# Tile-by-tile start, a 12-head last out-projection chunk and deadline-driven fillers in a one-core attention kernel

One core of one Trainium2 chip. The metric is the device time of one execution in microseconds. Profiles are of single executions; their spans run some 1.7 to 1.9 us under the times of the same executions.

## The reference

A LayerNorm without gain feeds two branches: attention of 32 heads over given key and value caches with an output projection, and an MLP with squared ReLU. Cut to what matters:

```python
# x: [2048, 512] bf16; k_cache, v_cache: [32, 2048, 128]; wq: [512, 4096]; wo: [4096, 512]
# w1: [512, 1792]; w2: [1792, 512]
xn = layernorm(x)
q = heads(xn @ wq)                                  # 32 heads of 128
p = softmax(q @ k_cache.T * 128 ** -0.5)
s = concat_heads(p @ v_cache) @ wo
g = silu(square(relu(xn @ w1 + b1)) @ w2 + b2)
out = x + s * g
```

## The kernel before

Queries are taken in four blocks of 512. A head of a block is eight *steps*; a step makes scores for two key tiles (2 matmuls of 512 columns), one exponential on ScalarE, and, two steps later, the product with V (8 matmuls of 129 columns, "PV"). Everything else of TensorE, called *fillers* here, is put between: projections of later heads (4 matmuls), MLP jobs (4 or 14), out-projection jobs over chunks of 8 heads. A credit counter spreads them. Cut, with `...` for what is left out:

```python
for i in range(TPB):                    # the four x tiles, all on SyncE
    ln_load(0, i)
fill_k(0)                               # a transposing DMA load, 512 KB
fill_wq(0, AC); fill_wq(1, AC); fill_v(0, AC); fill_wq(2, AC); fill_v(1, AC)    # ScalarE's queue
warm_up(10)
...                                     # norms on VectorE, transposes on TensorE
fill_k(1)
...                                     # w1 in four loads on SyncE, then b1 and b2 on GpSimd
for g in range(2):                      # heads 0 and 1 projected whole
    n, mm, evac = job_proj(g)
    for i in range(n):
        mm(i, g)
    t_bankF[g] = evac(g, 0)
t_b1 = E(DV, partial(_copy, out=b1f[:], in_=b1b[:]), deps=[tok_b1])
...
for pi in range(NPAIR):                 # 1024 steps
    gen_scores(pi)
    credit = min(credit + left[0] / (NPAIR - pi), 8.0)
    ...                                 # up to 2 or 3 fillers: fill_one(pi)
    if pi >= LAG:
        gen_pv(pi - LAG)
    ...
# last chunk of 8 heads: all heads but the last of every tile first, then the last heads
for i, (_, _, (n, mm, evac)) in enumerate(tail):
    for x in range(n - 1):
        mm(x, (places[i], waits[i]))
for i, (_, _, (n, mm, evac)) in enumerate(tail):
    mm(n - 1, (places[i], waits[i]))
    evac((places[i], waits[i]), step)
```

Names in the profiles: PE is TensorE (PEld its weight loads), DVE VectorE, ACT ScalarE, POOL GpSimd, SPq SyncE's queue of instructions. Tiles: `x_ln` x, `wq_sb` and `w_sb` weights (w1 and w2 are both `w_sb`), `kT` transposed keys, `v_sb` values, `qt_sb` projected queries, `oT` the transposed output of a head, which a transposing DMA makes. `psA`, `psF` and `psO`, in PSUM, are what the matmuls write: scores (2048 matmuls into `psA` in the page of the changed kernel), fillers (1460 into `psF`, the warm-up left out) and PV (8192 into `psO`). An *evacuation* is a copy out of PSUM. The *granted clock* is the share of TensorE's full speed that it was given. The *DMA share* adds up the packets' times over 16 DMA engines; it passes 1 (1.37 from 10 to 12 us in the kernel before).

The softmax here doesn't subtract the row's maximum and nothing guards it: scores larger than these inputs give would overflow.

Of the kernel before, what the change touches and what calls it, by code (L numbers as in the profile page):

```python
# [180 lines left out]

def _recip(e, out, in_):
    return e.reciprocal(out, in_)  # L183
# [36 lines left out]
def bass_recurrent_scan__mha_block_cached__dense_activation_squared_relu__prompt_kernel(  # L220
# [30 lines left out]
    NCH = H // HC  # L251
    LAG = 2
# [37 lines left out]
    mv_t = sb("mv_t", [P, TPB, 2], F32)  # L290
    ve_t = sb("ve_t", [P, TPB], F32)
# [31 lines left out]
    t_warm = E(GP, partial(_memset, out=warm[:], val=0.0))  # L323
# [15 lines left out]
    def ln_load(j, i):  # L339
        jt = j * TPB + i  # L340
        t_xl[jt] = S.emit_dma(
            SP, partial(_dma, out=x_ln[:, i, :], in_=A_x[0, jt * P:(jt + 1) * P, :]), sl_xl[i],
            deps=[t_xn.get(jt - TPB)])

    def ln_stats(j, i):
        jt = j * TPB + i
        prev = [t_xn.get(jt - TPB), t_xr.get(jt - TPB)]
        t = E(DV, partial(_bn_stats, out=st_t[:, i, :], in_=x_ln[:, i, :]),
              deps=[t_xl[jt]] + prev)
        t = E(DV, partial(_bn_aggr, out=mv_t[:, i, :], in_=st_t[:, i, :]), deps=[t])  # L350
        t = E(DV, partial(_ts, out=ve_t[:, i:i + 1], in0=mv_t[:, i, 1:2], scalar1=LN_EPS,
                          scalar2=None, op0=ALU.add), deps=[t])
        t_xr[jt] = E(GP, partial(_tt, out=rstd[:, i:i + 1], in0=ve_t[:, i:i + 1], in1=mhalf[:],
                                 op=ALU.pow), deps=[t, t_mhalf] + prev)

    def ln_scale(j, i):
        jt = j * TPB + i
        t_xn[jt] = E(DV, partial(_ts, out=xn_t[:, i, :], in0=x_ln[:, i, :],
                                 scalar1=mv_t[:, i, 0:1], scalar2=rstd[:, i:i + 1],
                                 op0=ALU.subtract, op1=ALU.mult),  # L360
                     deps=[t_xr[jt], t_xnr.get(jt - TPB)])
        if j > 0:
            t_xnr[jt] = tok_xT[j][i] = S.emit_dma(
                SP, partial(_dmaT, out=xnT[:, :, jt * P:(jt + 1) * P], in_=xn_t[:, i, :]),
                sl_xT[i], deps=[t_xn[jt]])
            return
        view = psA[:, i * 512:i * 512 + 256].bitcast(BF16)
        for c in range(NDC):
            t = E(PE, partial(_peT, out=view[:, c * P:(c + 1) * P],
                              in_=xn_t[:, i, c * P:(c + 1) * P], ident=ident[:]),  # L370
                  deps=[t_xn[jt], t_ident], inc=(c == NDC - 1))
        t_xnr[jt] = t
        tok_xT[0][i] = E(AC, partial(_act, out=xnT[:, :, i * P:(i + 1) * P],
                                     in_=view.rearrange("p (c q) -> p c q", q=P),
                                     func=ACT.Copy), deps=[t])

    def warm_up(n):
        for _ in range(n):
            E(PE, partial(_mm, out=bankF(1), lhsT=warm[:, 0:P], rhs=warm[:], start=True,
                          stop=True), deps=[t_warm], inc=False)  # L380
# [106 lines left out]
    def gen_oT(g):  # L487
        chunk = g // HC
        tok_oT[g] = S.emit_dma(
            SP, partial(_dmaT, out=oT[:, g % NOT, :].rearrange("p (t q) -> p t q", q=P),  # L490
                        in_=o_bf[:, g % 2, :, :].rearrange("p t d -> p (t d)")), sl_oT[g % 4],
            deps=[t_onorm[g], t_wodone.get(chunk - NOT // HC)])
# [47 lines left out]
    def job_h(j, c):  # L540
# [8 lines left out]
        def evac(bank, step):  # L549
            s = c % 2  # L550
            t1 = E(DV, partial(_ts, out=r_t[:, s, :], in0=bankF(bank), scalar1=b1f[:, c:c + 1],
                               scalar2=0.0, op0=ALU.add, op1=ALU.max),
                   deps=[box[0], t_b1, t_rt[s]])
            t_h2[j, c] = t_rt[s] = E(
                DV, partial(_tt, out=h2T[:, c, :], in0=r_t[:, s, :], in1=r_t[:, s, :],
                            op=ALU.mult),
                deps=[t1] + [t_o2.get((j - 1, qt)) for qt in range(TPB)])
            return t1
# [35 lines left out]
    def job_wo(j, m, qt):  # L594
        jt = j * TPB + qt
        g0 = j * H + m * HC
        box = [None]

        def mm(n, bank):
            g = g0 + n  # L600
            place, free = (bankF(bank), t_bankF[bank]) if isinstance(bank, int) else bank
            box[0] = E(PE, partial(_mm, out=place,
                                   lhsT=oT[:, g % NOT, qt * P:(qt + 1) * P],
                                   rhs=wo_all[:, m * HC + n, :], start=(n == 0),
                                   stop=(n == HC - 1)),
                       deps=[tok_wo[m], tok_oT[g], free], inc=(n == HC - 1))

        def evac(bank, step):
            if qt == TPB - 1:
                t_wodone[j * NCH + m] = box[0]  # L610
            if m == 0:
                t_acc[qt] = t = E(DV, partial(_copy, out=acc[:, qt, :], in_=bankF(bank)),
                                  deps=[box[0], t_fin.get(jt - TPB)])
            elif m < NCH - 1:
                t_acc[qt] = t = E(DV, partial(_tt, out=acc[:, qt, :], in0=bankF(bank),
                                              in1=acc[:, qt, :], op=ALU.add),
                                  deps=[box[0], t_acc[qt]])
                if m == NCH - 2:
                    at(step + 1, partial(pre_combine, j, qt))
            else:  # L620
                s = jt % 2
                place = bankF(bank) if isinstance(bank, int) else bank[0]
                t = E(DV, partial(_stt, out=tmp_t[:, s, :], in0=place, scalar=0.5,
                                  in1=g_all[:, jt % (2 * TPB), :], op0=ALU.mult, op1=ALU.mult),
                      deps=[box[0], t_g[jt], t_tmp[s]])
                t_fin[jt] = t_tmp[s] = E(
                    DV, partial(_tt, out=out_t[:, s, :], in0=tmp_t[:, s, :], in1=acc[:, qt, :],
                                op=ALU.add), deps=[t, t_u[jt], t_outdma[s]])
                eng, sl = (SP, sl_fin) if j == NQB - 1 else (GP, sl_out)
                t_outdma[s] = S.emit_dma(  # L630
                    eng, partial(_dma, out=out[0, jt * P:(jt + 1) * P, :], in_=out_t[:, s, :]),
                    sl[s], deps=[t_fin[jt]])
            return t
        return HC, mm, evac
# [19 lines left out]

    jobs = []
    for g in range(2, NG):
        jobs.append((NPR * (g - 2) - 2, NPR * (g - 2), job_proj(g)))
    for j in range(NQB):
        b = 10 + j * (SPB - NPR)
        for c in range(NFC):  # L660
            k = b + 6 + (SPB * 8 // 256) * c
            jobs.append((k, k - 40, job_h(j, c)))
        for qt in range(TPB):
            k = b + SPB // 2 - 4 + (SPB * 28 // 256) * qt
            jobs.append((k, k - 40, job_o2(j, qt)))
        b = j * SPB
        for m in range(NCH):
            for qt in range(TPB):
                r = b + HC * NPR * (m + 1) + 14
                jobs.append((r + 2 + 12 * qt, r, job_wo(j, m, qt)))  # L670
    tail_key = NPAIR + 14
    jobs.sort(key=lambda x: x[0])
    cur = [None]
    bank_no = [0]

    def fill_one(step, force=False):
        if cur[0] is None:
            for idx, (key, rel, job) in enumerate(jobs):
                if rel <= step or force:
                    cur[0] = [job, 0]  # L680
                    jobs.pop(idx)
# [6 lines left out]
        if i == n - 1:  # L688
            t_bankF[bank] = evac(bank, step)
            bank_no[0] ^= 1  # L690
            cur[0] = None
# [5 lines left out]
    for i in range(TPB):  # L697
        ln_load(0, i)
    fill_k(0)
    fill_wq(0, AC)  # L700
    fill_wq(1, AC)
    fill_v(0, AC)
    fill_wq(2, AC)
    fill_v(1, AC)
    warm_up(10)
    for i in range(TPB):
        ln_stats(0, i)
        if i >= 2:
            ln_scale(0, i - 2)
            warm_up(3)  # L710
    for i in range(TPB - 2, TPB):
        ln_scale(0, i)
        if i < TPB - 1:
            warm_up(2)
    fill_k(1)
    w1_view = B_w1.rearrange("(c p) f -> p c f", p=P)
# [10 lines left out]
    for g in range(2):  # L727
        n, mm, evac = job_proj(g)
        for i in range(n):
            mm(i, g)  # L730
        t_bankF[g] = evac(g, 0)
# [11 lines left out]
    for j in range(NQB):  # L743
        if j + 1 < NQB:
            for i in range(TPB):
                at(j * SPB + 3 * NPR, partial(ln_load, j + 1, i))
                at(j * SPB + 7 * NPR + 3 * i, partial(ln_stats, j + 1, i))
                at(j * SPB + 10 * NPR + 6 + NPR * i, partial(ln_scale, j + 1, i))
        at(j * SPB + SPB // 2, partial(load_xt, j))

    left = [sum(job[0] for _, _, job in jobs) - HC * TPB]
    credit = 0.0
    for pi in range(NPAIR):
        g, k = divmod(pi, NPR)
        gen_scores(pi)
        credit = min(credit + left[0] / (NPAIR - pi), 8.0)
        n = 0
        most = 3 if k == 2 else 2
        while n < most:
            late = bool(jobs) and jobs[0][0] + 8 <= pi  # L760
# [4 lines left out]
            if not fill_one(pi):  # L765
# [23 lines left out]
    tail = [x for x in jobs if x[0] >= tail_key]  # L789
    jobs = [x for x in jobs if x[0] < tail_key]  # L790
# [6 lines left out]

    assert len(tail) == TPB
    places = [bankF(bank_no[0]), bankF(bank_no[0] ^ 1), psA[:, 0:512], psA[:, 512:1024]]
    waits = [t_bankF[bank_no[0]], t_bankF[bank_no[0] ^ 1], t_exp[NPAIR - 2], None]  # L800
    for i, (_, _, (n, mm, evac)) in enumerate(tail):
        for x in range(n - 1):
            mm(x, (places[i], waits[i]))
    for i, (_, _, (n, mm, evac)) in enumerate(tail):
        mm(n - 1, (places[i], waits[i]))
        evac((places[i], waits[i]), step)
# [34 lines left out]
```

## Time and profile before

| | before |
|---|---|
| time, median of 3 (range) | 1254.86 us (1254.76 to 1255.04) |
| time of the profiled execution | 1252.6 us |
| span of the profiled execution | 1250.7 us |
| first score matmul / end of the last PV | 15.7 / 1233.7 us |
| last VectorE instruction ends | 1245.6 us |
| TensorE busy | 99% of the span |

To be read as three pieces: a front of 15.7 us, a loop in which TensorE is busy without a gap, and an end of 17.0 us. The lines are in the prediction. The profiled execution was 2.3 us faster than the three that were timed. In later runs the kernel before took between 1252.3 and 1255.5 us, by chip and by run, so each experiment is judged by its ratio to runs of the kernel before on its own chip.

### The profile page before, as it was taken

To read this page: it belongs to the slowest core of one execution; us is meant where nothing else is said; L and a number is where in the kernel's file an instruction comes from. 1 tells how busy PE (TensorE), PEld (TensorE's weight loads), DVE (VectorE), ACT (ScalarE), POOL (GpSimd) and SP (SyncE) were. 2 spreads that over 40 slices of the span, in tenths; PEclk is the share of its full clock that TensorE was granted. 3 is DMA by queue.
4 is the path that set the end of the run, shared out by engine and by line. 5 is a ranking of instruction groups with operands and counts; after the bars stand their busy time and mean duration, and the time that the engine had idled before them with its cause. 6 is when DMAs were issued, how large, how long until landed. Compare 5 with 4: busy or idle time off the path is not lost.

```text
span 1250.7 us, 26634 instructions
## 1 busy us (share of the span) xinstructions
PE 1235.7 (99%) x11746; PEld 812.1 (65%) x11746; DVE 473.5 (38%) x961; ACT 1051.3 (84%) x1045; POOL 27.6 (2%) x57
## 2 busy tenths in 40 slices
PE   8999999999999999999999999999999999999996
PEld 4666666666666666666666666666666666666664
DVE  3453333244435423324443542323443443333243
ACT  5888888888888888888888888888888888888884
POOL 1000000000001000000000100000000000000000
PEclk9999999999999999999999999999999999999999
DMA  9999987777888886777779889767877897788661
GB/s 233 205 217 218 163 146 143 133 133 143 147 165 153 155 150 129 143 146 133 135 146 172 149 143 161 136 131 141 146 132 144 151 163 130 134 149 134 132 118 30
DMA packets 686690, 185.39 MB, mean 148 GB/s; under 512 B 675152, under 2 KB 685648, under 8 KB 686576
## 3 DMA queue, kind: packets, MB, share of 16 engines
q1 hardware_dynamic: 679424, 178.44, 78.5%
q0 software_dynamic: 1440, 3.81, 1.2%
q10 hardware_dynamic: 5712, 1.44, 0.6%
q8 instruction: 93, 1.52, 0.5%
q14 instruction: 21, 0.17, 0.1%
HBM read 96.08 MB, written 2.10 MB: 78 GB/s over the span
## 4 chain that ended last, share of the span: by engine, by line
PE 98%; DVE 0%; DMA 0%; ACT 0%; issue 0%; SPq 0%
PE psO L157 37%; PE psA L152 36%; PE psF L152 25%; DMA x_ln<-in_A_x_dram 0%; DVE tmp_t L175 0%; DVE out_t L165 0%; PE psA L196 0%; SPq L208 0%; ACT pT L161 0%; DVE st_t L200 0%; ACT xnT L161 0%; DVE xn_t L171 0%; DVE mv_t L204 0%; DVE ve_t L170 0%
## 5 line engine op out<-in xcount | busy, mean ns | idle before, releaser
L161 ACT ACTIVATE pT<-psA 128x1024 bf16<-128x1024 f32 x1024 | 1040.9, 1023 | 171.9 <-PE psA L152 129.6
L157 PEld LDWEIGHTS psO<-v_sb,pT 128*128 128x128 bf16 x8192 | 548.3, 98 | 243.3 <-issue 9.5
L157 PE MATMUL psO<-v_sb,pT 128*128 128x129 bf16 x8192 | 633.3, 220 | 0.0
L152 PE MATMUL psA<-qt_sb,kT 128*128 128x512 bf16 x2048 | 609.2, 379 | 0.3 <-ACT pT L161 0.3
L179 DVE COPY o_un<-psO 128x258 f32<-128x258 f32 x256 | 97.3, 422 | 380.6 <-PE psO L157 379.9
L152 PE MATMUL psF<-xnT,wq_sb 128*128 128x512 bf16 x512 | 174.6, 379 | 0.8 <-ACT xnT L161 0.8
L152 PE MATMUL psF<-wo_all,oT 128*128 128x512 bf16 x496 | 164.8, 379 | 0.0
L152 PEld LDWEIGHTS psA<-qt_sb,kT 128*128 128x128 bf16 x2048 | 157.9, 98 | 1.6 <-ACT pT L161 0.7
L179 DVE CAST qt_sb<-psF 128x512 bf16<-128x512 f32 x128 | 88.2, 689 | 119.9 <-PE psF L152 119.9
L165 DVE TENSOR_TENSOR o_bf<-o_un,rden 128x512 bf16<-128x512 f32 x128 | 88.6, 692 | 4.4
L152 PEld LDWEIGHTS psF<-xnT,wq_sb 128*128 128x128 bf16 x512 | 50.0, 98 | 61.1 <-issue 0.9
L152 PEld LDWEIGHTS psF<-wo_all,oT 128*128 128x128 bf16 x496 | 48.5, 98 | 58.3
L152 PE MATMUL psF<-xnT,w_sb 128*128 128x512 bf16 x224 | 75.9, 379 | 0.0
L171 DVE TENSOR_SCALAR r_t<-psF,b1f 128x512 bf16<-128x512 f32 x56 | 42.0, 749 | 86.2 <-PE psF L152 86.2
L152 PE MATMUL psF<-w_sb,h2T 128*128 128x512 bf16 x224 | 73.8, 379 | 0.0
L152 PEld LDWEIGHTS psF<-xnT,w_sb 128*128 128x128 bf16 x224 | 21.9, 98 | 26.4
L152 PEld LDWEIGHTS psF<-w_sb,h2T 128*128 128x128 bf16 x224 | 21.9, 98 | 26.4
L165 DVE TENSOR_TENSOR acc<-psF,acc 128x512 f32<-128x512 f32 x32 | 22.0, 688 | 43.5 <-PE psF L152 43.5
L165 DVE TENSOR_TENSOR z_t<-psF,b2bc 128x512 f32<-128x512 f32 x16 | 11.1, 691 | 61.5 <-PE psF L152 61.5
L179 DVE COPY acc<-psF 128x512 f32<-128x512 f32 x16 | 11.0, 689 | 38.9 <-PE psF L152 38.9
L208 POOL DMA_DIRECT2D out_dram<-out_t x12 | 6.5, 541 | 856.9 <-DVE out_t L165 856.9
L183 DVE RECIPROCAL rden<-o_un 128x4 f32<-128x4 f32 x128 | 22.9, 179 | 4.4
(34 smaller groups left out, 156.3 us busy)
## 6 DMA issues: line engine op xcount, KB each, us to landing
v_sb<-in_A_v_cache_dram SPq DMA_DIRECT2D x126, 512.0 KB, 4.9
wq_sb<-in_A_wq_dram SPq DMA_DIRECT2D x125, 128.0 KB, 3.1
wo_all<-in_A_wo_dram SPq DMA_DIRECT2D x4, 1024.0 KB, 6.2
x_ln<-in_A_x_dram SPq DMA_DIRECT2D x16, 128.0 KB, 3.2
kT<-in_A_k_cache_dram SPq DMA_TRANSPOSE x128, 4.6
oT<-o_bf SPq DMA_TRANSPOSE x128, 4.0
x_t<-in_A_x_dram POOLq DMA_DIRECT2D x16, 128.0 KB, 4.0
w_sb<-in_B_w_dram SPq DMA_DIRECT2D x1, 1792.0 KB, 11.5
```

The costliest lines, as they stand in the source:

```text
L152: return e.matmul(out, lhsT, rhs, start=start, stop=stop)
L157: return e.matmul(out, lhsT, rhs, start=start, stop=stop, skip_group_check=True)
L161: return e.activation(out, in_, func, bias=bias, scale=scale)
L165: return e.tensor_tensor(out, in0, in1, op)
L171: return e.tensor_scalar(out, in0, scalar1=scalar1, scalar2=scalar2, op0=op0, op1=op1)
L179: return e.tensor_copy(out, in_)
L183: return e.reciprocal(out, in_)
L208: return e.dma_start(out, in_)
```

## The change

Its intent: start the scores earlier, by splitting the x loads over two issuing engines, sharing the norms between GpSimd, ScalarE and VectorE, and projecting head 0 tile by tile; and shorten the last VectorE chain, by making the last chunk 12 heads long and finishing it tile by tile. The core of the diff (cuts marked):

```diff
+    CH = [[(m * HC, (m + 1) * HC) for m in range(NCH)] for _ in range(NQB - 1)]
+    CH.append([(0, HC), (HC, 2 * HC), (2 * HC, 2 * HC + 4), (2 * HC + 4, H)])
 ...                                    # norm: variance + eps to GpSimd; tiles 0 and 1 scaled on ScalarE
     jobs = []
-    for g in range(2, NG):
-        jobs.append((NPR * (g - 2) - 2, NPR * (g - 2), job_proj(g)))
+    for g in range(1, NG):
+        jobs.append((NPR * g - 15, NPR * (g - 2), job_proj(g), g))
     for j in range(NQB):
-        b = 10 + j * (SPB - NPR)
+        b = 30 + j * (SPB - 6)
         for c in range(NFC):
-            k = b + 6 + (SPB * 8 // 256) * c
-            jobs.append((k, k - 40, job_h(j, c)))
+            k = b + (SPB * 9 // 256) * c
+            jobs.append((k, k - 130, job_h(j, c), None))     # key, earliest step, job
 ...
+    tail_order = [(0, x) for x in range(nt - 1)] + [(1, x) for x in range(nt - 3)]
+    tail_order += [(0, nt - 1)] + [(1, x) for x in range(nt - 3, nt)]
+    tail_order += [(i, x) for i in range(2, TPB + 1) for x in range(nt)]
 ...
-    for i in range(TPB):
-        ln_load(0, i)
+    ln_load(0, 0)
+    ln_load(0, 1, AC)
+    ln_load(0, 2)
+    ln_load(0, 3, AC)
+    fill_v(0)
+    fill_wq(0, AC)
     fill_k(0)
-    fill_wq(0, AC)
+    E(AC, partial(_act, out=th_t[:, 0, 0:1], in_=warm[:, 0:1], func=ACT.Exp), deps=[t_warm])
     fill_wq(1, AC)
-    fill_v(0, AC)
     fill_wq(2, AC)
-    fill_v(1, AC)
 ...                                    # transposes, copies and projections of head 0 by tile
     fill_k(1)
+    fill_v(1)                          # now ahead of w1 on SyncE
 ...
-    left = [sum(job[0] for _, _, job in jobs) - HC * TPB]
-    credit = 0.0
+    left = [sum(job[0] for _, _, job, _ in jobs) + 14]        # 14 of the last chunk in the loop
+    credit = 8.0
 ...
-        most = 3 if k == 2 else 2
+        most = 4 if pi < 2 else 3 if k == 2 else 2
```

## The prediction

> **What bounds the kernel now.** I read the page first (shares of the engines, chain), then the chain of work in order of time for the two ends, then the busy time by stretches, the groups and the waits.
>
> ```profile
> PE 1235.7 (99%) x11746; PEld 812.1 (65%) x11746; DVE 473.5 (38%) x961; ACT 1051.3 (84%) x1045; POOL 27.6 (2%) x57
> ...
> PE 98%; DVE 0%; DMA 0%; ACT 0%; issue 0%; SPq 0%
> ```
>
> TensorE is the bound and nearly the whole chain. The question is what lies in the ends, so a stretch of the trace, from the first score matmul to the end of the last PV matmul:
>
> ```profile
> core 0: us, PE busy (x) PEld busy (x) DVE busy (x) ACT busy (x) POOL busy (x), PEclk, DMA share, GB/s
> 15.71:1233.70 1217.99, 1217.74 (x11671) 804.54 (x11672) 459.29 (x930) 1047.64 (x1040) 21.61 (x40) 1.00 0.82 149
> ```
>
> The loop takes 1218.0 us, of which PE is busy 1217.7. That leaves 15.7 us ahead of it and 17.0 behind it (1250.7 - 1233.7). I then took the distance between the starts of the score pairs in the trace, by the number of "filler" matmuls (projections, MLP, out-projection) between them: 0.885 us with none, 1.101 with one, 1.317 with two, 1.532 with three. So a step costs 0.885 us and each filler 0.216, without exception; no step is longer because ScalarE (1.023 us a step) was late. The loop is rigid: its time is the number of its matmuls. All that can be won lies in the two ends, 32.7 us together.
>
> ```profile
> 2.13 5.93 DMA x_ln<-in_A_x_dram
> 8.09 0.70 DVE st_t L200
> ...
> 13.07 0.61 ACT xnT L161
> 13.81 1.89 PE psF L152 x8
> 15.71 0.61 PE psA L152 x2
> ```
>
> Start, in the chain (start, us, what): the fourth x tile lands at 8.06; its norm, transposes and copies end at 13.68; two heads are projected whole (8 matmuls) before the first scores at 15.71. The tile view of kT shows a second condition: its first load is issued at 2.6 and needs 10.4 us, landing at 13.0.
>
> ```profile
> 1233.92 3.02 PE psF L152 x14
> 1236.94 3.02 PE psA L152 x14
> ...
> 1240.22 0.70 DVE tmp_t L175
> ```
>
> End: 28 out-projection matmuls run while the last oT is made (the trace has it issued at 1235.46 and landed at 1237.94), then 4 more, then four times two VectorE instructions of 0.69 us, ending at 1245.6; the last store lands 1.7 us later (1247.4) and 3.3 us of closing work follow.
>
> [...] the warm-up matmuls are 0.43 us apart at first, 0.216 later, and the granted clock is 0.50 in the stretch 10 to 12 us after PE idled for some 2.7 us of the stretch before. [...] with both issuing, the stretch 0 to 10 us has a DMA share of 0.99, 10 to 12 us 1.37. [...] here one load of 1283 ns begins at 5.76 and ended before the first copy, so moving it forward by a dummy exp is worth at most tenths.
>
> **The change, part by part.**
>
> *Start, compute path.* x goes out in two issues on each of two engines. The first two tiles landed at 3.39 and 4.35 before; all four should land by about 4.6. VectorE: bn_stats 0.69 + aggregate 0.18 + gaps = 0.94 a tile, so aggregates at 4.3, 5.3, 6.2, 7.2. GpSimd gets the rest: the power op 0.57 (0.563 row), and three small ops that no row shows; I estimate 0.2 to 0.3 each. Tiles 0 and 1 need all four (1.2 to 1.5), tiles 2 and 3 two of them (0.8 to 0.9): GpSimd ends about 4.4 + 1.35 + 1.35 + 0.85 + 0.85 = 8.8. Then scale 0.41, transposes 0.5, copy 0.60, four projections of 128 columns 0.4, half an evacuation 0.4, gaps 0.3: first scores at 11.4 against 15.7. It also drops head 1's projection (4 x 0.216) from the front into the loop.
>
> *Start, kT.* The load now stands behind two x tiles and a V load, but the second V load (512 KB) no longer competes. Ahead of kT's end lie x 512, V 512, three wq 384 and kT 512 KB = 1.9 MB; at the 206 to 233 GB/s of those stretches that is 8.5 us from about 2, plus landing: 11 or so. Level with compute, hence no further delay in the middle case.
>
> *The wait that takes its place: w1.* I stepped the diff's credit counter (counts only; the same counter on the old rule gives 48, 543, 410 and 23 steps of 0, 1, 2, 3 fillers, as the trace has). The first step now takes 4 fillers (head 1), the next 3 and the third 3, of which the second is already the first MLP matmul. PE reaches it after 6 score and 8 filler matmuls, 14 x 0.216 = 3.0 us after the first scores: at 14.4. Before, w1's first quarter was issued at 12.3 and landed 5.5 later, at 17.8, and the first MLP matmul ran at 19.17 after just as much loop work (3.0 us). In the new order the second V load is ahead of w1 on SyncE's queue; the bytes ahead of w1's end are the same 3.6 MB. If the queue runs without the hole that it had, at 250 GB/s with 15 of them, it lands at 15 to 16. I take 15.2, a stall of 0.8 us. The loop is then ahead of before by 19.17 - 15.2 = **4.0 us**.
>
> *Loop.* By the counter 1434 fillers stand in it against 1432: +2 x 0.216 = **+0.4**.
>
> *The oT of head 30.* The last chunk is now 12 heads, and tile by tile. By the counter 14 of its matmuls fall in the loop, and the 11th (head 30) in step 1020 of 1023. Before, that oT was issued 1.70 us after the PV of step 1017 ended (1226.04) and landed 4.1 after it. PE now comes there after a step of 1.101, one of 0.885 and a score pair of 0.43, 2.4 us after it: a stall of **+1.7**, inside the loop where nothing hides it.
>
> *Tail.* After the last PV (T) 6 matmuls remain that don't need the last head: 1.3 us. The last oT lands at T + 4.2 as before (1237.94 - 1233.7), so PE idles 2.9 us. Then 1 + 3 + 12 + 12 matmul equivalents, 28 x 0.216 = 6.05, to T + 10.3; VectorE and the first three tiles' stores run beside them. The last half tile then needs 0.16 of pipeline, 2 x 0.38, 1.7 of store and 3.3 of closing work: T + 16.3 against T + 17.0: **-0.7**. The final VectorE chain of 5.4 us shrinks to 0.8, but 24 matmuls (5.2 us) have come after the last oT in exchange for it.
>
> Sum: -4.0 + 0.4 + 1.7 - 0.7 = -2.6; time 1254.86 - 2.6 = **1252.3 us**.
>
> **Rivals.**
> 1. *The start gains nothing, DMA holds it.* If w1 lands at 17.8 as before (same bytes), PE waits there until then, and the loop is ahead by 1.4 instead of 4.0: about 1255. For it: DMA share near or above 1 for the first 20 us. Against: the queue had holes, such as kT's first load 10.4 us in flight.
> 2. *The clock cools in the tail.* [...] the stretch before showed 0.50 granted after about as much. Half clock for 3.4 us costs up to 1.7 us of the final 6: 1254.
> 3. *Start and tail both clean.* If w1 is there in time (4.8 instead of 4.0), and head 30's oT lands before it is needed because the norm starts earlier, the change is worth 0.8 + 1.7 more: 1249.8. For it: the parameters (14 matmuls, 12 heads, a first credit of 8) look as if somebody had tried them. If the tail's oT lands earlier too, somewhat under.
> 4. *Slower by ScalarE.* Fillers bunched so that it becomes the bound. Against: by the counter there are 24 steps without a filler instead of 48, never two in a row.
>
> **Range and chances.** The start is worth 1.4 to 4.8, the end between +3 and -2.5; both together put the time between about 1248.5 and 1255.5 in 8 of 10 cases. The ends hold 32.7 us of which at most half is movable, so 25 us (2%) is out of reach either way: faster by over 2% 0.01, within 2% 0.98, slower 0.01.
>
> **What would show it.** Right: a first score matmul near 11.4; the first MLP matmul waiting for w1 near 15; steps still 0.885 + 0.216 n; a PE gap of about 1.7 us before a psF matmul of wo_all some 5 us before the last PV; a PE gap of 2 to 3 us after it; VectorE ending under 1 us after PE. Wrong: no PE gap at w1 (start worth more) or one of 3 us (worth less); a granted clock of 0.5 after the tail's gap; a kT landing after 12 that holds the scores.

What rival 2 compares with is the tail's idle of 2.9 us, and its half clock for 3.4 us is there in the trace of the kernel before: 0.50 from 9.35 to 12.76 us. The forecast: its sum came to -2.6 us, from -4.0, 0.4, 1.7 and -0.7, so 1252.3 us. The 0.2 to 0.3 us for three small GpSimd operations was a guess without a row of the trace behind it; the changed kernel's trace has 0.19 each.

## The result

The changed kernel took 1258.17 us, the median of 4 runs (1256.59 to 1259.58), beside 1254.88 for the kernel before. The ratio is 1.0026 (95% interval 1.0008 to 1.0043). It is 3.3 us slower, where 2.6 us faster was predicted, and outside the range.

The waits of TensorE in the changed kernel, from the view of who waited for whom (us in total, times, longest):

```profile
PE psF L152 <- DMA w_sb<-in_B_w_dram: 4.4, 1, 4.4
PE psF L152 <- DMA oT<-o_bf: 4.3, 2, 2.7
...
PE psA L152 <- DMA kT<-in_A_k_cache_dram: 1.0, 1, 1.0
```

None of the three is in the kernel before, whose front waited on norms and copies. Now the same stretches in time (us, then busy time of PE, PEld, DVE, ACT and POOL with counts, granted clock, DMA share, GB/s):

```profile
12.03:15.23 3.20, 3.19 (x14) 1.29 (x14) 0.00 (x0) 2.23 (x3) 0.00 (x0) 1.00 1.19 173
15.23:19.68 4.45, 0.01 (x1) 0.01 (x1) 1.36 (x3) 0.84 (x1) 0.00 (x0) 0.90 1.24 277
19.68:25.86 6.18, 6.18 (x33) 3.67 (x34) 1.18 (x2) 1.84 (x2) 0.00 (x0) 0.52 1.14 295
1233.60:1235.30 1.70, 0.17 (x2) 0.01 (x1) 0.00 (x0) 1.26 (x2) 0.00 (x0) 1.00 0.40 77
1240.30:1244.56 4.26, 1.51 (x11) 0.55 (x8) 1.63 (x4) 0.00 (x0) 0.00 (x0) 0.95 0.16 31
1244.56:1252.30 7.74, 7.71 (x40) 4.19 (x40) 3.74 (x6) 0.00 (x0) 2.53 (x2) 0.81 0.10 34
```

First row: scores begin at 12.03, 3.7 us earlier than before, and 14 matmuls run. Second: TensorE stands still for 4.45 us, for w1. Third: its clock is at 0.52 for 6 us after it. Fourth: the wait for head 30's oT. Fifth and sixth: the gap in the tail, and a lowered clock after it too.

The chain of work says what the front is made of now (start, us, what); before, it ran through the x loads, norms and matmuls, and now it is one queue:

```profile
2.12 6.79 SPq L220
8.91 0.05 issue
8.96 2.83 SPq L220
11.79 0.04 issue
11.83 0.58 SPq L216
12.41 0.04 issue
12.46 7.17 DMA w_sb<-in_B_w_dram
```

SyncE spends 6.79 us issuing the first kT load (5.09 before), 2.83 on the second, then issues the second V load, then w1 at 12.46, which takes 7.17 us to land, at 19.63. Before, it was issued at 12.30 and landed at 17.8; the second V load was on ScalarE's queue then. Whether this made the difference is tested in v1_act: by itself it did not.

The two spans differ by 7.1 us (1257.8 less 1250.7), more than the 3.3 us between the medians: the profiled execution was the slowest of the four (1.4 us over their median), and that of the kernel before 2.3 us under its own. By the distances between score pairs, as in the prediction:

| piece | predicted | in this trace |
|---|---|---|
| first scores, 15.71 before | 11.4 (-4.3) | 12.03 (-3.7) |
| wait at w1 | +0.8 | +4.45 |
| lowered clock after that wait (three steps too long by 0.98, 1.27, 0.83) | none | +3.1 |
| two more fillers | +0.4 | +0.4 |
| wait for head 30's oT | +1.7 | +1.7 |
| not assigned, up to the last PV | | +0.6 |
| from the last PV to the end, 17.0 before | -0.7 | +0.45 |
| sum | about -2.6 | +7.1 |

(The predicted rows add to -2.1: the prediction reckoned its front from the first MLP matmul, 19.17 to 15.2, and not from the first scores.)

### The profile page after: what moved, and what is told of

It reads as the page before. It is cut to its first block, busy times and chain, and to the rows that moved or that the text cites. A ratio compares the mean times of both kernels' runs of the same rounds, so it can differ in the third digit from the quotient of the medians.

```text
span 1257.8 us, 26666 instructions
## 1 busy us (share of the span) xinstructions
PE 1240.5 (99%) x11772; PEld 812.8 (65%) x11755; DVE 471.9 (38%) x946; ACT 1056.8 (84%) x1047; POOL 33.7 (3%) x78
## 4 chain that ended last, share of the span: by engine, by line
PE 97%; DMA 1%; SPq 1%; DVE 0%; issue 0%
PE psO L157 37%; PE psA L152 35%; PE psF L152 25%; SPq L220 1%; DMA w_sb<-in_B_w_dram 1%; DMA oT<-o_bf 0%; SPq L216 0%; DVE o_un L179 0%; DVE o_bf L165 0%; DVE tmp_t L175 0%; DVE out_t L165 0%; DVE rden L191 0%
## 5 line engine op out<-in xcount | busy, mean ns | idle before, releaser
L152 PE MATMUL psF<-wo_all,oT 128*128 128x512 bf16 x488 | 167.9, 381 | 4.3 <-DMA oT<-o_bf 4.3
L152 PE MATMUL psF<-xnT,wq_sb 128*128 128x512 bf16 (+1 forms) x524 | 168.6, 374 | 0.2 <-ACT xnT L161 0.2
L179 DVE CAST qt_sb<-psF 128x512 bf16<-128x512 f32 (+1 forms) x129 | 88.2, 684 | 111.4 <-PE psF L152 111.4
L152 PE MATMUL psF<-xnT,w_sb 128*128 128x512 bf16 x224 | 78.5, 385 | 4.4 <-DMA w_sb<-in_B_w_dram 4.4
L165 DVE TENSOR_TENSOR h2T<-r_t 128x512 bf16<-128x512 bf16 x56 | 23.8, 425 | 1.9
```

The source lines that it names most:

```text
L152: return e.matmul(out, lhsT, rhs, start=start, stop=stop)
L165: return e.tensor_tensor(out, in0, in1, op)
L179: return e.tensor_copy(out, in_)
```

## The experiments

Sixteen kernels ran, all correct. Times are medians of 4 runs.

### The wait at w1: three loads, one behind the other

**w1_early** puts w1's first quarter ahead of the second kT and V loads.

```diff
-    fill_k(1)
-    fill_v(1)
     w1_view = ...
     for i, (c0, c1) in enumerate([(0, 4), (4, 8), (8, 11), (11, 14)]):
+        if i == 1:
+            fill_k(1)
+            fill_v(1)
         tok_w1[i] = ...
```

> The changed kernel with one edit: the first quarter of w1 is issued ahead of the second kT and the second V load. Theory (w1's late landing, through its place in the queue, is what cost the start): it lands near 14 instead of 19.6, PE waits under 0.5 us at the first MLP matmul instead of 4.4, and the clock does not fall to half after it (3.1 us); about 7 us less than the changed kernel's 1258.2, so 1251. Rival (the DMA engines are saturated, so whatever goes first only moves the wait to the second kT or V): PE waits as long at step 8 or 10, and the time stays within 1.5 us of 1258. Rival 2 (the loss is in the tail alone): no change.

Measured: 1257.07 us (1256.28 to 1262.27), ratio 1.0035. The theory's first half held: w1 landed at 13.6. Its second half fell: TensorE waited 9.3 us, for something else. From the waits, and from the timeline (start, us, engine, instruction, idle before it and its releaser), of the execution that took 1262.3 us:

```profile
PE psF L152 <- DVE qt_sb L179: 9.3, 1, 9.3
```

```profile
23.31 0.17 DVE L179 CAST b1f<-b1b 128x14 f32<-128x14 bf16 x1 [11.67 <-DMA b1b<-in_B_b_dram]
23.40 1.28 DVE L179 CAST qt_sb<-psF 128x512 bf16<-128x512 f32 x2
```

The cast of b1 stands on VectorE ahead of two evacuations. It waits for b1, so the PSUM banks stay full and the first MLP matmul has no bank. In the changed kernel that wait was there too (the cast ran at 15.3, the first evacuation ended at 16.0), hidden behind w1; the kernel before has evacuated heads 0 and 1 before the cast. What b1's landing at 23.3 went with is shown by two stretches of the same run (GB/s last, DMA share before it):

```profile
13.00:14.00 1.00, 1.00 (x7) 0.45 (x5) 0.00 (x0) 0.73 (x2) 0.00 (x0) 1.00 1.27 272
14.00:23.00 9.00, 0.97 (x5) 0.24 (x3) 0.00 (x0) 1.76 (x2) 0.00 (x0) 0.78 1.30 51
```

The engines stay busy (share 1.30) and move 51 GB/s instead of 272, for 9 us, while kT and GpSimd's loads of b1 and b2 are in flight together. This execution was the slowest; the other three took 1256.3 to 1257.4 us, and no trace of them was kept.

**late_mlp** leaves the loads and holds MLP jobs back to step 6.

```diff
-            jobs.append((k, k - 130, job_h(j, c), None))
+            jobs.append((k, max(k - 130, 6), job_h(j, c), None))
```

> The changed kernel with one edit: the first MLP jobs are not released before step 6 instead of step 2; the DMA order is as in the changed kernel, w1 still lands near 19.6. Theory (PE waits because it reaches w1 too early): PE does scores and PV of steps 3 to 5 (3 x 1.05 us, ScalarE-bound, without fillers) in the time that it waited; the wait falls from 4.4 to about 0.5 to 1 us and the half clock does not come; 1252. Rival (DMA-bound start): V or kT waits take its place and the time stays near 1258.

Measured: 1257.17 us (1255.08 to 1258.27), ratio 1.0025. Its waits:

```profile
PE psF L152 <- DMA wq_sb<-in_A_wq_dram: 2.9, 1, 2.9
...
PE psF L152 <- DMA w_sb<-in_B_w_dram: 1.0, 1, 1.0
```

The 1.05 us a step of ScalarE is what nine exponentials in a row, 9.47 us, took in the changed kernel's tail. The wait at w1 fell to 1.0 as expected, but the wq load of head 3, which lies behind all of w1 in the queue, took its place, and a half clock came later, at 25.6. The rival was right about this edit: reordering TensorE's work did not help while the loads stayed in that order (ratio 1.0025 beside 1.0026 to 1.0035).

**v1_act** puts the second V load back on ScalarE's queue.

```diff
     fill_wq(2, AC)
+    fill_v(1, AC)
 ...
     fill_k(1)
-    fill_v(1)
```

> The changed kernel with one edit: the second V load goes back to ScalarE's queue behind the wq loads, where the kernel before had it. Theory (the 512 KB ahead of w1 on SyncE's queue are what made w1 later than before): w1's first quarter lands near 17.8 as before instead of 19 to 19.6, the wait falls by 1 to 2 us; kT may land later (13 as before) and take back up to 1 us; the time 1 to 2.5 us under the changed kernel's. Rival (only the bytes count, whichever queue): w1 lands at 19 or later and the time stays within 1 us of the changed kernel's.

Measured: 1257.34 us (1256.23 to 1258.62), ratio 1.0033, beside 1.0035 for the changed kernel on the same chip. w1 landed at 19.4 all the same, and kT only at 15.3, so that scores waited 4.2 us for it. The rival holds: where the V load stood only decided who waited. It is not the place of this one load alone that makes w1 late.

**start_fixed** reorders three things: b1 and b2 are issued by GpSimd first of all, while it has nothing to do; w1's first quarter goes ahead of the second kT; the rest of w1 is issued from steps 2, 8 and 12, so behind wq, kT and V of the next head.

```diff
+    tok_b1 = S.emit_dma(GP, ...)       # moved here from behind the norms
+    tok_b2 = S.emit_dma(GP, ...)
     ln_load(0, 0)
 ...
+    load_w1(0)
     fill_k(1)
     fill_v(1)
-    ...                                # all four w1 loads
+    at(2, partial(load_w1, 1)); at(8, partial(load_w1, 2)); at(12, partial(load_w1, 3))
```

> The changed kernel with the loads of its start in another order: b1 and b2 issued by GpSimd while it waits for the first norms (their cast stands ahead of two evacuations on VectorE, which the run with w1 alone brought to light), w1's first quarter ahead of the second kT, its other quarters from the loop. Theory (two waits stood behind each other at the first MLP matmul, w1's landing and the evacuation held by the b1 cast): both go, PE reaches and runs the first MLP matmul near 15.0, no wait over 0.5 us there, clock 1.00 after it; 7 us less than the changed kernel, 1251 where the kernel before takes 1254.9 (ratio 0.997). Rival (the start is bound by the bytes themselves): a wait of 2 to 4 us on another load (wq, kT or V) within the first 25 us, ratio near 1.002.

Measured: 1252.31 us (1250.62 to 1255.02), ratio 0.9986 (0.9969 to 1.0003). No wait for w1, wq or an evacuation is left; the first MLP matmul runs at 15.96; the clock stays full until the end (mean granted clock of the execution 0.999). What remains is kT, which landed at 12.9 in this profile and held the scores 2.1 us. So the theory stands with a smaller gain: 5 to 6 us of the 7, by the difference of the two ratios (1.0026 to 1.0035 less 0.9986), and the 2.1 us at kT are the rival's share. The three moves were made together; what each is worth was not measured, only that w1 alone (w1_early) is not enough.

### The clock

**warm_gaps** fills both waits with dummy matmuls and removes none.

```diff
+            if j == 0 and c == 0 and n == 0:         # before the first MLP matmul
+                for x in range(18):
+                    E(PE, ...warm..., deps=[t_warm, t_bankF[bank]], inc=False)
 ...
+        if (i, x) == (0, nt - 1):                    # before the last head is needed
+            for y in range(10):
+                E(PE, ...warm into a free bank..., inc=False)
```

> The changed kernel with 18 dummy matmuls (3.9 us) on PE before the first MLP matmul and 10 (2.2 us) before the first matmul that needs the last head's oT; all waits stay as they are, they are only filled. Theory (half the loss at w1, and the loss of the tail, is the clock that cools in the idle): the granted clock stays at 1.00 in both places, 3.1 us are won at the start and 1.2 at the end; about 1254. Rival (the half clock has nothing to do with these idle times): no change, 1258, half clock still there. If the dummies overrun a wait, some tenths are lost.

Measured: 1255.73 us (1255.25 to 1255.83), ratio 1.0015. The stretches that answer to rows two, three and the last of the changed kernel:

```profile
15.36:20.14 4.78, 3.89 (x18) 0.19 (x2) 1.36 (x3) 0.84 (x1) 0.00 (x0) 1.00 1.23 281
20.14:25.00 4.86, 4.86 (x48) 3.20 (x47) 1.18 (x2) 2.97 (x3) 0.00 (x0) 1.00 1.18 306
1242.30:1248.50 6.20, 6.20 (x40) 3.80 (x40) 4.23 (x6) 0.00 (x0) 2.54 (x2) 1.00 0.12 42
```

The waits are no shorter than they were, the clock is 1.00 in all of them, and 48 matmuls pass in 4.86 us where 33 passed in 6.18. The last 40 take 6.2 us instead of 7.7. So here the idle time is what lowered the clock: 0.52 and 0.81 behind the waits left idle, 1.00 behind the filled ones. In time it is worth 1.4 to 2.5 us (ratios 1.0026 and 1.0035 less 1.0015; the intervals overlap, so the traces are the better witness), not 4: the profiled run of the changed kernel was its worst, and the dummies ran 0.4 us past w1's landing at 19.76. The runs also lie within 0.6 us of each other instead of 3.

**after_again**, the changed kernel once more, gave the yardstick.

> The changed kernel itself, unaltered, as the yardstick of this call's chip. Ratio to the kernel before 1.001 to 1.004, with its own runs up to 3 us apart (they were 1256.6 to 1259.6)[...].

Measured: 1257.45 us (1257.05 to 1258.55), ratio 1.0035. In its profile the clock fell after the wait at w1 (half for 6.8 us) but not in the tail, where the gap was as long; from the last PV to the end it then took 16.0 us, where the prediction had 16.3.

What went with a lower clock in one execution and not in another, after the same gap, was read from the kept traces. In each of the 18, the granted clock changed only at instants that lie whole multiples of 3.41 us apart (18.77, 25.59, 1244.15 and 1247.57 in the changed kernel's). Cut the traces into these stretches of 3.41 us: up to the last matmul, the full clock fell at the end of each stretch in which TensorE had been busy for 40% or less (16 of them), and of none in which it had been busy for 44% or more. Three of the 16 are in the two kernels' own traces: 0.00 us busy from 15.36 to 18.77 and 1.07 from 1240.74 to 1244.15 in the changed kernel, 1.04 from 5.94 to 9.35 in the kernel before. So in these traces the fall went with where the gap lay in this grid. The stretch at whose end the clock fell, and the emptiest one of after_again around its gap:

```profile
1240.74:1244.15 3.41, 1.07 (x5) 0.29 (x3) 1.22 (x4) 0.00 (x0) 0.00 (x0) 1.00 0.20 38
1239.52:1242.93 3.41, 1.77 (x14) 0.80 (x12) 1.63 (x4) 0.00 (x0) 0.00 (x0) 1.00 0.06 11
```

Eight of the traces have the tail's gap of 2.75 us. In four (the changed kernel, head30, late_mlp, v1_act) the clock fell, and from the last PV to the end took 17.3 to 17.7 us; in the other four (w1_early, start_fixed, after_again, w1_early_b2late) it took 16.0.

### The tail

**head30** moves one matmul.

```diff
-    tail_order = [(0, x) for x in range(nt - 1)] + [(1, x) for x in range(nt - 3)]
-    tail_order += [(0, nt - 1)] + ...
+    tail_order = [(0, x) for x in range(nt - 2)] + [(1, x) for x in range(nt - 3)]
+    tail_order += [(0, nt - 2), (0, nt - 1)] + ...
```

> The changed kernel with one edit: the matmul of head 30 of the first tile comes after nine matmuls of the second tile instead of before them, so still 14 in the loop but none that needs a late oT. Theory: the wait of 1.5 to 1.7 us in step 1020 goes and nothing takes its place; 1.6 us less than the changed kernel, 1256.6 (ratio 1.0013). Rival (the wait was beside ScalarE's end and hidden): no change, 1258.2 (ratio 1.0026).

Measured: 1256.87 us (1256.54 to 1256.94), ratio 1.002. Of two waits for oT (4.3 us) one is left (2.7). The time agrees with the theory to 0.3 us; the intervals of the ratios overlap, so the trace is the better witness.

**tail_fill** leaves 13 more matmuls of the last chunk for the gap behind the loop.

```diff
-    left = [sum(job[0] for _, _, job, _ in jobs) + 14]
+    left = [sum(job[0] for _, _, job, _ in jobs) + 1]
```

> The changed kernel with one edit: 1 matmul of the last chunk in the loop instead of 14, so 19 instead of 6 are left to fill the wait for the last oT, and head 30's oT is not needed inside the loop. Theory: the 1.7 us wait at step 1020 goes; the loop is 13 x 0.216 = 2.8 us shorter and the gap of 2.75 us is filled with that work; the clock does not fall in the tail (1.2 us); less about 1 us because the last 18 steps with half a filler each become ScalarE-bound. Together 4.5 us less than 1258.2: 1253.7. Rival (the tail is bound by the chain after the last oT whatever comes before): only the 1.7 us, 1256.5.

Measured: 1252.55 us (1252.17 to 1253.7), ratio 0.9994, so some 4 to 5 us under the changed kernel. Both waits for oT are gone. Its end in the chain of work:

```profile
1233.92 0.63 PE psO L157 x8
1234.55 5.11 PE psF L152 x23
1239.65 5.22 PE psA L152 x36
1244.88 0.02 issue
1244.90 0.44 DVE tmp_t L175
```

In the tail TensorE goes through without a gap and without a half clock (23 matmuls in 5.11 us, 0.22 us each, where at half clock behind the changed kernel's wait at w1 two took 0.85); the wait at w1 is still there (4.3 us). Work that is there to fill a wait had been done ahead of it, in a loop where TensorE was already full.

**tail_old** takes the chunks and the order of the kernel before into the changed kernel (the last tile stays in halves, two additions stay on GpSimd).

```diff
-    CH.append([(0, HC), (HC, 2 * HC), (2 * HC, 2 * HC + 4), (2 * HC + 4, H)])
+    CH.append([(m * HC, (m + 1) * HC) for m in range(NCH)])
 ...
+    tail_order = [(i, x) for i in range(TPB + 1) for x in range(nt - 1)]
+    tail_order += [(i, nt - 1) for i in range(TPB + 1)]
 ...                                    # and none of it in the loop: + 14 taken out of left
```

> The changed kernel with the last out-projection chunk as before (four chunks of 8 heads, all heads but the last of every tile first, then the last heads; none of it in the loop; the last tile stays in two halves). Theory (the tail of the change costs 1.7 us at head 30, 0.4 of two more fillers and 0.4 behind the last PV, of which 1.2 is half clock): 2.5 us less than the changed kernel, 1255.7 (ratio 1.0005). Rival (the tail of the change is a gain and the whole loss is at the start): at least 1 us more than the changed kernel.

Measured: 1257.01 us (1256.93 to 1257.08), ratio 1.0021: about 1 us under the changed kernel, not 2.5. It is not a clean undo: the span from the last PV to the end was 17.6 us, since GpSimd's addition takes 1.26 us where VectorE's takes 0.69, and the additions after it waited for an earlier store (1.90 us on GpSimd, 0.94 on VectorE). The rival (the tail of the change is a gain) did not hold either.

### Both, and what the rest is worth

**start_tail** is start_fixed with the edit of tail_fill.

> The same start with the one edit of the tail run (1 instead of 14 matmuls of the last chunk in the loop). If the two losses are separate they add: 7 + 5 = 12 us less than the changed kernel's 1258.2, 1246 where the kernel before takes 1254.9 (ratio 0.993). If the start's wait was bound elsewhere: 1252 to 1253 (ratio 0.998 to 1.0).

Measured: 1248.17 us (1246.35 to 1249.22) where the kernel before took 1254.26: ratio 0.9949 (0.9934 to 0.9964). It is faster than both kernels, by 0.5% on the kernel before; the two repairs add up to within their noise. Its waits of TensorE, the warm-up's start and the norms (2.2 us together) left out:

```profile
PE psA L152 <- DMA kT<-in_A_k_cache_dram: 1.2, 1, 1.2
...
PE psO L157 <- ACT pT L161: 0.2, 1, 0.2
```

**x_one_queue** puts the four x loads of start_tail back on SyncE.

```diff
-    ln_load(0, 1, AC)
+    ln_load(0, 1)
 ...
-    ln_load(0, 3, AC)
+    ln_load(0, 3)
```

> The kernel of start_tail with the four x loads all on SyncE again, as in the kernel before. Theory (the split loads are worth nothing by themselves: GpSimd's chain of small operations, some 0.9 to 1.5 us a tile, and kT pace the start, not x): the fourth x tile lands some 0.5 to 1 us later, the last projection is evacuated within 0.5 us of 11.4, the time is that of start_tail within 0.7 us (ratio 0.995). Rival (the split is what makes the start short): 1 us or more later.

Measured: 1247.02 us (1246.56 to 1248.34), ratio 0.9952. The fourth x tile landed at 6.37 instead of about 4.3, and head 0's projection was evacuated at 11.40 in both: the split is worth nothing here. It hides behind kT, for which the scores wait 1.2 us in both, and behind GpSimd's chain, for whose results the norms waited 4.9 us in the changed kernel (2.9 on ScalarE, 2.0 on VectorE); the chain took 1.4 us a tile for the first two tiles and 0.8 for the others there.

**kt_first** issues kT ahead of V in start_tail.

```diff
+    fill_k(0)
     fill_v(0)
     fill_wq(0, AC)
-    fill_k(0)
```

> The kernel of start_tail (both repairs) with the first kT load ahead of the first V load. Theory: kT lands near 10 instead of 11.9 and the first scores start when the projection is evacuated, 11.5 instead of 12.1 to 13; V lands near 13 and is first needed near 14.9; 0.6 us less than start_tail, ratio 0.994 where start_tail had 0.995. Rival: V or w1 comes late in its place, then 0.5 us more than start_tail.

Measured: 1254.28 us (1253.63 to 1256.85), ratio 1.0012. kT landed at 16.5, not at 10: neither side had foreseen that. The stretch in which b1 and b2 are in flight beside it:

```profile
5.00:6.50 1.50, 1.45 (x7) 0.00 (x0) 1.47 (x4) 0.62 (x1) 1.17 (x5) 1.00 1.32 203
6.50:14.00 7.50, 3.64 (x37) 1.99 (x34) 2.21 (x7) 2.68 (x5) 2.12 (x7) 1.00 1.36 69
```

Again a high DMA share, 1.36, at a third of the bytes (69 GB/s after 203). Three runs were to tell whether b2's load, a row broadcast to 128 partitions, is the cause. All three emit it from step 24 of the loop (`at(24, load_b2)`), with b1 left where each had it.

**w1_early_b2late**

> The run with w1's first quarter moved ahead, and b2's load taken out of the start. Theory (the broadcast of b2 beside a transposing load is what slowed everything from 14 to 23 us): b1 lands near 15, the second kT near 16 to 17, the wait at the first MLP matmul falls from 9.3 us to 0.5 to 1.5 (behind the b1 cast), the clock may stay full; 3 to 6 us under w1_early, ratio 0.998 to 1.001. Rival (w1 ahead of kT is what slowed it): the wait stays over 4 us, ratio 1.003.

**kt_first_b2late**

> kt_first with b2's load taken out of the start. Theory: kT lands near 8 to 10 instead of 16.5, the first scores start when the projection is evacuated, 11.5, V lands before 14; ratio 0.994 (start_tail 0.995, kt_first 1.001). Rival (kT beside other queues is slow whatever they carry): kT lands at 13 or later, ratio 0.997 or more.

**start_tail_b2late**

> start_tail with b2's load taken out of the start, the yardstick of the other two. Theory: there the b2 load met the first V load and only the beginning of kT, so it cost little: kT lands 0.5 to 1 us earlier, the first scores start near 11.5, ratio 0.9945. Rival: no change, 0.995.

The edit did not do what it was meant to. GpSimd waited for nothing of the loop here: it issued b2 as soon as it came to it, at 9 to 10.4 us. So w1_early_b2late is w1_early again: 1252.72, 1259.84, 1252.78 and 1259.49 us, two kinds of run; in its profiled one (1252.7) b1 landed at 16.2 and the wait was 2.4 instead of 9.3. What decides its kind of run is not known. start_tail_b2late gave 1248.03 us, ratio 0.9956, no change. kt_first_b2late gave 1253.91 us, ratio 0.9999; in it b2's packets came only from 14 us on, and kT landed at 15.8 all the same. So b2 is not the cause there.

**kt_first_borig** is kt_first with b1 and b2 issued behind the norms, as the changed kernel has them.

> kt_first with b1 and b2 issued where the changed kernel does it, after the norms. Theory (b1's gather beside kT is the cause): kT lands by 10, the first scores start near 11.5. The b1 cast then lets the evacuations wait until about 15, so a wait of about 1 to 3 us before the first MLP matmul; ratio 0.995 to 0.997. Rival (kT beside the wq loads[...] is slow by itself): kT lands at 13 or later, and ratio 0.999 or more.

Measured: 1251.88 us (1251.82 to 1252.12), ratio 0.999. kT landed at 11.2 and the scores began at 11.48; in the stretch that answers to the slow one, 231 GB/s are moved at about the same share (1.34):

```profile
5.00:6.50 1.50, 1.07 (x5) 0.00 (x0) 0.84 (x3) 0.70 (x1) 1.17 (x5) 1.00 0.20 8
6.50:11.00 4.50, 3.64 (x37) 1.99 (x34) 2.54 (x7) 2.60 (x5) 3.88 (x9) 1.00 1.34 231
```

That speaks for b1's gather of single elements beside a kT load as what slowed the transfers, and against the wq loads of ScalarE's queue, which are there in both. kT's 11.2 lies between what the two sides expected (10 and 13), and moving b1 also moved GpSimd's other work, so I call it possible and not shown. Against it: in the changed kernel b1's load (issued at 9.1, landed at 15.3) and the second kT load (9.0 to 16.2) were in flight together too, and 179 GB/s moved from 12 to 16 us. The wait then moved to w1 (2.4 us) and wq (1.6).

## Why the prediction was wrong

**Right.** The loop is rigid (steps of 0.885 + 0.216 a filler in the changed kernel's trace too), and the two ends are all there is. The compute path of the front: 11.4 predicted for head 0's projection, 11.45 measured. GpSimd's small operations took 0.19 us each where 0.2 to 0.3 was guessed. kT "level with compute": 11.99, a wait of 1.0, of which 0.6 beyond the projection. The first MLP matmul reached 3.0 us after the first scores: 3.2. Head 30's oT: 1.7 and 1.7, and head30 took the wait away. The tail's gap: 2.9 and 2.75; from the last PV to the end 16.3 (its terms add to 16.2), and 16.0 in the executions whose clock stayed full.

**Wrong, the step that failed:** "If the queue runs without the hole that it had, at 250 GB/s with 15 of them, it lands at 15 to 16." The landing of w1 was mis-sized: the term of 0.8 us measured 4.45. The bytes were about right (3.6 MB said; both traces move 3.97 MB until w1 lands). The rate was not. All loads from 2 us to w1's landing, in the kernel before and in the changed one (the last figure is GB/s):

```profile
2.00:17.81 15.81, 12.02 (x49) 4.85 (x48) 6.78 (x19) 5.14 (x7) 4.71 (x10) 0.89 1.21 246
2.00:19.63 17.63, 11.34 (x65) 3.29 (x48) 6.52 (x16) 7.87 (x10) 5.58 (x14) 0.98 1.14 221
```

So 250 GB/s was near what the kernel before had. The new order moved less, 221, where a landing at 15.2 needs about 300. A hole did not close, one opened: from 10 to 12 us 118 GB/s moved, where the kernel before had 233. ScalarE's loads had all landed by 9.2, and V and w1 were still to be issued (11.83 and 12.46), behind SyncE's 6.79 and 2.83 us in the issue of two kT loads. That this hole is the whole of the loss is not shown: v1_act, with V on ScalarE's queue, moved 226 GB/s, and w1 landed at 19.4. What is shown is that w1's landing changed with the order of the loads: ahead of the second kT it came at 13.6 (w1_early), and in start_fixed the wait was gone. The step's own sum was also early: 3.6 MB at 250 GB/s are 14.4 us, and begun at 2 us, as in its sum for kT, they end at 16.4. Rival 1, which took 17.8 for w1, still chose too early.

**Missed altogether:** what 4.45 us of idle did to the clock. I gave that rival to the tail alone, where the gap was 2.9 us, because I had made the first wait small. It cost 3.1 us in the profiled execution; warm_gaps shows that the idle is its cause. In the tail it came in four of eight traces, as that rival said; after and after_again, one and the same kernel, got one each.

**Not seen:** the cast of b1 ahead of two evacuations, and wq behind w1. Neither shows in the changed kernel's time, since both lie within the wait at w1. But they are why w1_early and late_mlp, each right about its own wait, won next to nothing. The intended gain of the front (3.7 us earlier scores) was real and was spent before 20 us: it ended at a queue of loads which no part of the change had made shorter.

**Open:** why the loads, with kT and GpSimd's small loads in flight together, fell to a fifth to a third of the bytes (51 GB/s after 272 in w1_early, 69 after 203 in kt_first), and why only in some executions; and why the kernel before moved the same 3.97 MB 1.8 us sooner.

## What to carry to other kernels

When a front is made shorter on the compute side, list every load that the first microseconds of the new order need, with its place in its queue and its landing time, and do not carry over the rate of the old order: here it fell from 246 to 221 GB/s when the order changed. A gap on TensorE cost more than its length where the clock fell after it: 4.45 us at w1, and 3.1 more. A wait found by the profile may hide others that end earlier; change the order of all of them at once, or the time won goes to the next. And count the work left to fill a known gap: doing 13 matmuls of it early, in a loop that was already full, made the loop longer and left the gap empty here (4 to 5 us, by tail_fill).
